# A new order in the projections of a gated mix of two attentions: products, exponentials, splits and copies change places

## The chip, the cores and the metric

The kernel runs on one core of one Trainium2 chip. A core has a matrix engine (TensorE, PE in the profile; its weight loads are PEld), a vector engine (VectorE, DVE), a scalar engine (ScalarE, ACT), a general engine (GpSimd, POOL) and a queue engine that issues transfers (SyncE, SP). Each engine works through its own instructions in order and waits where an operand or a buffer is not ready. The metric is the time of one execution in device microseconds, the median of the runs of a kernel.

## The reference

The input is one sequence x of 2048 tokens with 512 features, in float32. Two attentions with 32 heads of 16 features are computed of it and mixed by a gate.

```python
x = A_x
g = _sigmoid((x * gate_w).sum(-1, keepdims=True))
a = _A_ref(x, A_wqkv, A_wo)               # softmax over all 2048 keys, then @ wo
b = _B_ref(x, B_wq, B_wk, B_wv, B_wo, B_beta)
return g * a + (1 - g) * b

# _B_ref, four segments of 512 tokens:
for s in range(N):
    logits = jnp.einsum("bhqd,bhkd->bhqk", qs, ks) * scale + mask
    a_dot = softmax(logits) @ vs
    pq = phi(qs)                            # phi(t) = t + 1 where t > 0, else exp(t)
    num = jnp.einsum("bhld,bhde->bhle", pq, M)
    den = jnp.einsum("bhld,bhd->bhl", pq, z)[..., None] + 1e-6
    outs.append(sigmoid(beta) * num / den + (1 - sigmoid(beta)) * a_dot)
    pk = phi(ks)
    M = M + jnp.einsum("bhld,bhle->bhde", pk, vs)
    z = z + jnp.einsum("bhld->bhd", pk)
```

A is a full softmax attention. B has a local softmax within each segment of 512 tokens and a memory M, z, that each segment's queries read and each segment's keys and values then add to. The first segment finds the memory empty.

## The kernel before

**Two stages.** The first stage, the projections, makes q, k and v of both attentions, the memory's products and the gate. It lasts for the first 303 us of the profile. The main stage follows: scores (L1056), maxes of scores (L242, reduced on DVE at L275 and L290), exponentials (ACT, L1079), sums over values (L155), and at the end the output projection. The change lies in the first stage alone.

**Slots.** The first stage is a list of slots. A slot is 12 matmuls of 128x128 by 128x512: four steps of depth 128, each with three products of halves. A float32 operand is split into a high half (a cast on ACT) and a low half (a subtraction on DVE or POOL; `split`, L399 to L403), and of the four products of halves the one of low by low is left out. The function `slot` (L377) issues three matmuls, then whatever functions are posted for place 0, then three more and place 1, and so on to place 3. So the order of the work on every engine is written by hand, as slot and place: `post(slots, place, f)` counts from the present slot, `post_at(n, place, f)` names it. Nothing else orders the work; the engines wait for each other by semaphores, and for a buffer by the tile that it reuses (a tag has so many buffers: q1 and q2 three, ph four, full and am two, mn, ex and dn one).

**A's keys and values.** Each pair of chunks of 512 tokens goes through Strassen and Winograd's seven products p1 to p7 (the table `ORDER`, L453; `v_pair` and `k_pair`). S1 to S4 are sums of blocks of x (`s_sum`, L594), T1 to T4 sums of blocks of weights (`t_sum`, L605), and each is split in two halves. In the first `v_pair` the eight tiles of A's queries fill slots 4 to 11, between p2 and the third product. Then come `k_pair` at slot 22 and 29 and two more pieces of `v_pair` to slot 49. With S0 = 50 begin 32 slots of B's q and k tiles, four of q and four of k for each of the four segments.

**A q or k tile** (`qk_tile`, L411). After its slot, ACT copies the bank to the tile full (L426), casts q1 out of it (L427), and POOL makes mn = min(full, 0) (L431); at the next place DVE makes the low half q2 (L434) and, where phi is wanted, ACT makes ex = exp(mn) (L438); one slot on DVE makes ph = max(full, 0) + ex (L443).

**The memory.** `mem_k` transposes a tile of phi(k) (L841, copied by ACT at L843), `mem_k2` multiplies it with v (L855), `mem_k3` adds to the running memory on DVE (L862 to L866). `mem_q` multiplies phi(q) with the memory into four banks, num (L814), and one, den (L818). ACT copies the num banks to tiles (L824) and SP stores them to numd (L825). These tiles take the tags full and am in turn, so they share full's two buffers with the q and k tiles.

**Maxes.** `some_max` does a set of four maxes of the main stage early: four matmuls (L242) into the banks sm, and four reductions on DVE (L275); 96 maxes, 24 sets, are done so. num uses the banks of the same tag sm.

**Gate.** `load_gate` brings four tiles of x's rows, `gate_logit` (L777) sums them on DVE, and `gates` (L899 to L906) transposes the logits, takes the sigmoid and stores them to gd.

**Rows of ones.** Each of the ten tiles of keys gets two small transfers of ones (L765), issued by POOL's queue.

Of the kernel before, what the change touches and what calls it, by code (L numbers as in the profile page):

```python
# [22 lines left out]
CH = 512  # L23
# [24 lines left out]
def gated_mix(ctx, tc, x, xT, wqkv, a_wo, b_wq, b_wk, b_wv, b_wo, beta, gate_w, out):  # L48
# [284 lines left out]
    with ExitStack() as p0:  # L333
# [78 lines left out]
        def qk_tile(w, xc, o, dst, then=None, side="B", bank=None, low=V):  # L412
# [20 lines left out]
            def e1():  # L433
                low.tensor_sub(q2, full, q1.bitcast(F32))  # L434
                store(1, q2)
                if then:
                    ph["ex"] = wk1.tile([128, CH], F32, tag="ex", name="ex")
                    nc.scalar.activation(ph["ex"], ph["mn"], AF.Exp)  # L438
# [7 lines left out]
            post(0, 1, e1)  # L446
            post(1, 1, e2)
# [5 lines left out]
        ORDER = (("p1", "11", "11"), ("p2", "12", "21"), ("p6", "S2", "T2"), ("p7", "S3", "T3"), ("p5", "S1", "T1"),  # L453
# [60 lines left out]
        def v_pair(xo, cs, bs, fill=None, tags=("full", "full", "am", "am")):  # L514
# [42 lines left out]
            for p, x, w in ORDER:  # L557
                x, w = xo[x], vops[w]
                if fill and p == "p6":
                    fill()  # L560
                prods = []
                for b, xb, yb in zip(bs, xbanks, ybanks):
                    if p == "p1":
                        X[b] = xb()
                    elif p in ("p2", "p7"):
                        Y[b] = yb()
                first = p in ("p1", "p2", "p7")
                outer = fill and p in ("p1", "p2")
                order = [(b, k, a, c) for k in range(2) for a, c in ((0, 0), (0, 1), (1, 0)) for b in bs] if outer else \
                    [(b, k, a, c) for b in bs for k in range(2) for a, c in PARTS]  # L570
                left = {b: 6 for b in bs}
                for i in range(0, len(order), 12):
                    part = order[i:i + 12]
                    prods = []
                    for m, (b, k, a, c) in enumerate(part):
                        ps = X[b] if p in ("p1", "p6", "p5", "p3") else Y[b]
                        left[b] -= 1
                        prods.append((ps, x[a][k][:, b * 128:(b + 1) * 128], w[c][k], first and left[b] == 5, left[b] == 0))
                        if left[b] == 0:
                            post(0, m // 3, lambda p=p, b=b: done(p, b))  # L580
                    slot(prods, not first)
# [57 lines left out]
        for n, place, f in ((6, 3, lambda: t_sum("T1", *vb, V)), (7, 0, lambda: t_sum("T3", *vb, P)),  # L639
                            (7, 1, lambda: s_sum("S1", x0, x1, V)), (7, 2, lambda: t_sum("T2", *vb, V)),  # L640
                            (7, 3, lambda: s_sum("S3", x0, x1, P)), (8, 2, lambda: s_sum("S2", x0, x1, V)),
                            (9, 0, lambda: t_sum("T4", *vb, P)), (9, 1, lambda: op_split(vops["T2"], vr[1][2:4], P)),
                            (9, 2, lambda: op_split(xo0["S2"], x0, V)), (10, 0, lambda: s_sum("S4", x0, x1, V)),
                            (10, 1, lambda: op_split(xo0["S3"], x1, V)), (10, 3, lambda: op_split(vops["T3"], vr[1], P)),
                            (11, 1, lambda: op_split(xo0["S1"], x1[2:4], V)), (11, 3, lambda: op_split(xo0["S4"], x0[2:4], V)),
                            (12, 2, lambda: late_op("T1", 2, vr[0][0:2])), (13, 2, lambda: late_op("T4", 3, vr[0][2:4]))):
            post_at(n, place, f)
# [14 lines left out]
        post_at(14, 1, load_k_raw)  # L662
# [41 lines left out]
        for n, place, f in ((18, 3, a22), (19, 2, lambda: s_sum("S1", x2raw, x3raw, V)),  # L704
                            (19, 3, lambda: s_sum("S3", x2raw, x3raw, P)),
                            (24, 2, lambda: plain("11", 7, x2raw[0:2])), (25, 0, lambda: s_sum("S2", x2raw, x3raw, V)),
                            (25, 2, lambda: plain("12", 9, x2raw[2:4])), (26, 0, lambda: s_sum("S4", x2raw, x3raw, V)),
# [32 lines left out]
        staged(xchunk(1), xcs, 1, at_u(8), (6, 10), (47, 0), [(53 + k, 0) for k in range(KT)], P)  # L740
        staged(xchunk(2), xcs, 2, at_u(2), (3, 4), (S0 + 4, 0), [(S0 + 9 + k, 0) for k in range(KT)], P)
        staged(xchunk(3), xcs, 3, at_u(8), (7, 10), (S0 + 10, 0), [(S0 + 17 + k, 0) for k in range(KT)], P)
# [37 lines left out]
        def load_gate(c):  # L780
            t = unit4((3, 7, 2, 2)[c], F32)
# [27 lines left out]
        def mem_q(c):  # L809
# [11 lines left out]

            def keep(i):
                am = wk.tile([128, CH], F32, tag=("full", "am")[i % 2], name="am", bufs=2)
                nc.scalar.copy(am, banks[i])  # L824
                nc.sync.dma_start(numd[c][i], am)  # L825
# [55 lines left out]
        for n in range(36, S0):  # L881
# [3 lines left out]
            elif n > 37:  # L885
                post_at(n, 3, some_max)
# [4 lines left out]
        for n in range(32):  # L891
            if n in (14, 22, 30):
                post_at(S0 + n, 3, lambda c=n // 8: mem_q(c))
            elif n % 2 == 0:
                post_at(S0 + n, 3, some_max)

        def gates():
            gps = me_ps.tile([128, CH], F32, tag="me", name="gps")
            nc.tensor.transpose(gps[:16, :128], glog, identf)  # L899
            gt = wk1.tile([128, 4, 128], F32, tag="ex", name="gt")  # L900
# [437 lines left out]
    n = 0  # L1338
# [81 lines left out]
```

## Time and profile before

| what | value |
|---|---|
| runs | 1770.07, 1770.28, 1775.54 us; median 1770.28 us |
| the profiled execution's own time | 1768.32 us |
| its span, first to last instruction | 1766.5 us |
| mean granted clock of TensorE | 0.995 |
| busy share of the span | PE 98%, PEld 50%, DVE 91%, ACT 82%, POOL 44% |
| first stage, 0 to 303.1 us: busy | PE 277.01, DVE 205.88, ACT 159.17, POOL 143.61 us |
| 400 to 800 us: busy | PE 400.00, DVE 399.78, ACT 356.85, POOL 177.83 us |

The shares over the span are nearly all main stage, in which PE and DVE are busy without a gap. The first stage is read by itself, from the busy times of stretches, from the waits of each engine within it, and from PE's timeline, in which a number in brackets is the idle time ahead of an instruction and the engine and line that ended it. The chain that ended last has 92% of the span in PE.

### The profile page before, as it was taken

What the parts mean: (1) busy time and instruction counts of PE and PEld (TensorE: products, weight loads), DVE (VectorE), ACT (ScalarE), POOL (GpSimd) and SP (SyncE); (2) the same over time, 40 slices, a digit from 0 to 9 for tenths busy, and PEclk for the clock granted to TensorE, in tenths of its full rate; (3) what the DMA queues carried; (4) which work ended last, traced back from release to release, by engine and by line L of the source; (5) the groups of instructions that cost most, each with busy time, mean ns of one, the idle gap of its engine ahead of it and who ended that gap; (6) DMA issues with size and microseconds to landing.
All of it is one profiled execution on the core that took longest, in us unless ns stands there. A gap on an engine that the chain in (4) does not pass through costs nothing.

```text
span 1766.5 us, 41587 instructions
## 1 busy us (share of the span) xinstructions
PE 1735.9 (98%) x15157; PEld 880.9 (50%) x15157; DVE 1599.9 (91%) x3321; ACT 1445.3 (82%) x2779; POOL 770.4 (44%) x1014
## 2 busy tenths in 40 slices
PE   8999988999999999999999999999999999999999
PEld 7876655544444444444444444444444444444444
DVE  7658765999999999999999999999999999999931
ACT  6553546888888888888888888889889888888884
POOL 3533663415162527453445344353434353535343
PEclk9999999999999999999999999999999999999999
DMA  6568876444363436544444444444544444544551
GB/s 234 178 231 222 286 236 206 129 108 137 113 169 107 132 120 183 147 139 137 132 138 127 147 129 147 129 137 115 151 119 146 129 136 124 148 125 142 140 166 62
DMA packets 168507, 264.97 MB, mean 150 GB/s; under 512 B 39496, under 2 KB 80488, under 8 KB 168304
## 3 DMA queue, kind: packets, MB, share of 16 engines
q1 hardware_dynamic: 166720, 260.91, 49.4%
q8 instruction: 121, 1.98, 0.5%
q0 software_dynamic: 1440, 1.14, 0.3%
q14 instruction: 82, 0.67, 0.1%
q10 hardware_dynamic: 144, 0.26, 0.1%
HBM read 177.74 MB, written 83.25 MB: 148 GB/s over the span
## 4 chain that ended last, share of the span: by engine, by line
PE 92%; POOL 2%; ACT 2%; issue 1%; DVE 1%; DMA 1%; SPq 0%; ACTq 0%; POOLq 0%; DVEq 0%
PE ops L155 40%; PE st L1056 27%; PE sm L242 14%; PE pr L385 6%; PE pair L385 2%; PE sm L155 2%; POOL mn L431 1%; DMA numd<-am 1%; POOL u L403 0%; PE mt_ps L232 0%; ACT u L402 0%; PE sm L1056 0%; ACT full L426 0%; PE idle L346 0%; ACT pt L843 0%
## 5 line engine op out<-in xcount | busy, mean ns | idle before, releaser
L1079 ACT ACTIVATE p<-st 128x512 f32<-128x512 f32 x2261 | 1190.9, 601 | 146.9 <-PE sm L242 91.1
L275 DVE TENSOR_REDUCE pm<-sm 128x1 f32<-128x512 f32 x2048 | 1276.9, 684 | 12.1 <-PE sm L242 11.5
L242 PE MATMUL sm<-kA,qA 48*128 48x512 f32 x2048 | 661.4, 424 | 2.3 <-DMA kA<-kdA 2.3
L1056 PE MATMUL st<-qA,kA 50*128 50x512 f32 x2014 | 657.5, 432 | 3.2 <-ACT full L426 3.2
L155 PE MATMUL ops<-p,vA 128*17 128x256 f32 (+3 forms) x6360 | 552.9, 445 | 0.0
L1056 PEld LDWEIGHTS st<-qA,kA 50*128 50x128 f32 x2014 | 327.4, 185 | 426.9 <-ACT p L1079 382.3
L242 PEld LDWEIGHTS sm<-kA,qA 48*128 48x128 f32 x2048 | 338.0, 185 | 12.9 <-issue 2.8
L1180 POOL TENSOR_TENSOR rcp<-rec,minus 128x32 f32<-128x32 f32 x43 | 234.8, 5461 | 78.8 <-DMA rec<-dend 73.1
L290 DVE CUSTOM_DVE_ANT_0 rest<-sm,mask 128x128 f32<-128x128 f32 (+3 forms) x512 | 246.9, 482 | 0.4 <-PE sm L242 0.4
L155 PEld LDWEIGHTS ops<-p,vA 128*17 128x17 f32 x6360 | 129.3, 96 | 214.9 <-issue 183.9
L1060 POOL TENSOR_SCALAR_AFFINE_SELECT p<-p 128x512 f32<-128x512 f32 x128 | 79.4, 636 | 269.4 <-ACT p L1079 264.9
L242 PE MATMUL sm<-kB,qB 48*128 48x128 f32 (+3 forms) x512 | 166.5, 385 | 0.0
L385 PE MATMUL pr<-u,u 128*128 128x512 f32 x392 | 103.4, 403 | 12.7 <-ACT full L426 12.6
L1056 PE MATMUL st<-qB,kB 50*128 50x512 f32 (+1 forms) x495 | 105.4, 329 | 0.3 <-ACT mt L235 0.3
L1056 PEld LDWEIGHTS st<-qB,kB 50*128 50x128 f32 x495 | 68.6, 186 | 62.2 <-ACT p L1079 50.4
L385 PEld LDWEIGHTS pr<-u,u 128*128 128x128 f32 x392 | 72.9, 191 | 33.2 <-ACT full L426 15.2
L155 PE MATMUL ops<-p,vB 128*17 128x128 f32 (+3 forms) x1504 | 88.3, 350 | 0.2 <-ACT part L1270 0.2
L214 POOL TENSOR_TENSOR dm<-pm 128x32 f32<-128x32 f32 x32 | 7.6, 239 | 172.1 <-DVE pm L275 172.1
L242 PEld LDWEIGHTS sm<-kB,qB 48*128 48x128 f32 x512 | 80.2, 185 | 0.0
L434 DVE TENSOR_TENSOR q<-full,q 128x512 fp32r<-128x512 f32 x40 | 32.2, 805 | 33.9 <-ACT q L427 30.7
L223 POOL CAST ms<-pm 128x16 fp32r<-128x16 f32 x32 | 6.3, 196 | 126.7 <-DVE pm L290 126.6
L431 POOL TENSOR_SCALAR mn<-full 128x512 f32<-128x512 f32 x24 | 40.2, 1674 | 38.1 <-ACT full L426 37.8
(230 smaller groups left out, 1496.1 us busy)
## 6 DMA issues: line engine op xcount, KB each, us to landing
kA<-kdA SPq DMA_DIRECT2D x256, 128.0 KB
vA<-vdA SPq DMA_DIRECT2D x31, 544.0 KB
kA<-kdA SPq DMA_DIRECT2D x256, 64.0 KB
qB<-qdB SPq DMA_DIRECT2D x192, 64.0 KB
kB<-kdB SPq DMA_DIRECT2D x192, 64.0 KB
kdA<-q SPq DMA_DIRECT2D x32, 256.0 KB
qA<-qdA SPq DMA_DIRECT2D x64, 128.0 KB
qdB<-q SPq DMA_DIRECT2D x32, 256.0 KB
```

The lines of the kernel that those rows point to most:

```text
L155: behind[0] = nc.tensor.matmul(*args, **kw)
L214: nc.gpsimd.tensor_sub(dm, pm[:, :, :, 2:4], pm[:, :, :, 0:2])
L242: nc.tensor.matmul(ps[:, n0:n0 + n], rows(qt[u][:, :, s * 128:(s + 1) * 128], h, 48), rows(k[:, :, k0:k0 + n], h, 48), start=True, stop=True)
L275: nc.vector.tensor_reduce(pm[:, h, s, kc:kc + 1], ps, axis=AX.X, op=ALU.max, negate=True)
L290: nc.vector.tensor_tensor_reduce(out=tri["rest"][:, 0:w], in0=ps[:, n0:n0 + w], in1=tri["mask"][:, CH - w:], scale=-1.0, scalar=3.0e38, op ...
L385: nc.tensor.matmul(ps, l, r, start=start, stop=stop, skip_group_check=chained)
L431: nc.gpsimd.tensor_scalar_min(ph["mn"], full, 0.0)
L434: low.tensor_sub(q2, full, q1.bitcast(F32))
L1056: nc.tensor.matmul(ps[:, n0:n0 + CH - q0], rows(k[:, :, b * 128:(b + 1) * 128], h, 50), rows(q[:, :, q0:], h, 50), start=True, stop=True)
L1060: nc.gpsimd.affine_select(out=x, in_=x, pattern=[[0, 4], [1, 128]], base=0, channel_multiplier=-1, compare_op=ALU.is_ge, fill=0.0)
L1079: nc.scalar.activation(p[:, h], ps, AF.Exp, scale=SCALE)
L1180: eng.tensor_tensor(r, rec, minus, op=ALU.pow)
```

## The change

Nothing that is computed changes, and no product is added or left out. What changes is the place of the work, and at four points its engine, its tile or its bank:

- The third of the seven products is p7 (S3 by T3), then p6 (S2 by T2). S and T sums and their splits get new slots and places to match, and S3's sum goes from POOL to DVE.
- In the first `v_pair`, p1 and p2 no longer end all four banks in the last four matmuls: the first half of the depth is done for all banks, then the second half bank by bank. The queries take their banks in the other order.
- The load of raw k, one plain split and one sum move by a slot or a place; the sets of maxes begin at slot 39, not 38, and the 13 sets within the last 32 slots stand at every even slot from 0 to 24.
- phi's exponential moves from place 1 to place 3, behind the next tile's copy and cast.
- The low halves of x's chunks 1, 2 and 3 move from POOL to DVE and from place 0 to place 2; chunk 3 is loaded four slots later, into other tiles.
- The twenty transfers of ones go to SP's queue.
- Two of the loads of gate rows come later and into other tiles; the gates are made at slot 26 of the 32, not 30, and in the tag gw, not ex.
- The memory's products leave by four tiles of their own, not by full and am, and `mem_q` stands one slot earlier, at 13, 21 and 29.

```diff
             def e1():
                 low.tensor_sub(q2, full, q1.bitcast(F32))
                 store(1, q2)
+
+            def e1x():
                 if then:
                     ph["ex"] = wk1.tile([128, CH], F32, tag="ex", name="ex")
                     nc.scalar.activation(ph["ex"], ph["mn"], AF.Exp)
...
             post(0, 1, e1)
+            post(0, 3, e1x)
             post(1, 1, e2)
...
-        ORDER = (("p1", "11", "11"), ("p2", "12", "21"), ("p6", "S2", "T2"), ("p7", "S3", "T3"), ("p5", "S1", "T1"),
+        ORDER = (("p1", "11", "11"), ("p2", "12", "21"), ("p7", "S3", "T3"), ("p6", "S2", "T2"), ("p5", "S1", "T1"),
                  ("p3", "S4", "22"), ("p4", "22", "T4"))
...
-                if fill and p == "p6":
+                if fill and p == "p7":
                     fill()
...
-                order = [(b, k, a, c) for k in range(2) for a, c in ((0, 0), (0, 1), (1, 0)) for b in bs] if outer else \
+                order = [(b, 0, a, c) for a, c in ((0, 0), (0, 1), (1, 0)) for b in bs] + \
+                    [(b, 1, a, c) for b in bs for a, c in PARTS] if outer else \
                     [(b, k, a, c) for b in bs for k in range(2) for a, c in PARTS]
...
-                            (7, 3, lambda: s_sum("S3", x0, x1, P)), (8, 2, lambda: s_sum("S2", x0, x1, V)),
...
+                            (7, 0, lambda: t_sum("T3", *vb, P)), (7, 1, lambda: s_sum("S3", x0, x1, V)),
+                            (7, 3, lambda: op_split(xo0["S3"], x1, V)), (8, 0, lambda: op_split(vops["T3"], vr[1], P)),
...
-        post_at(14, 1, load_k_raw)
+        post_at(15, 0, load_k_raw)
...
-        staged(xchunk(2), xcs, 2, at_u(2), (3, 4), (S0 + 4, 0), [(S0 + 9 + k, 0) for k in range(KT)], P)
-        staged(xchunk(3), xcs, 3, at_u(8), (7, 10), (S0 + 10, 0), [(S0 + 17 + k, 0) for k in range(KT)], P)
+        staged(xchunk(2), xcs, 2, at_u(2), (3, 4), (S0 + 4, 0), [(S0 + 9 + k, 2) for k in range(KT)], V)
+        staged(xchunk(3), xcs, 3, at_u(2), (10, 8), (S0 + 14, 0), [(S0 + 18 + k, 2) for k in range(KT)], V)
...
-                post_at((S0 - 10 if i < 4 else S0 + 10) + i, 1 + 2 * r, lambda t=t, r=r: nc.gpsimd.dma_start(
+                post_at((S0 - 10 if i < 4 else S0 + 10) + i, 1 + 2 * r, lambda t=t, r=r: nc.sync.dma_start(
...
-                    qk_tile(wq8, xq, o, qd["A", o, c], side="A", bank=(me_bank, pr_bank)[o // 2])
+                    qk_tile(wq8, xq, o, qd["A", o, c], side="A", bank=(pr_bank, me_bank)[o // 2])
...
+            ams = unit4(7, F32)
+
             def keep(i):
-                am = wk.tile([128, CH], F32, tag=("full", "am")[i % 2], name="am", bufs=2)
-                nc.scalar.copy(am, banks[i])
-                nc.sync.dma_start(numd[c][i], am)
+                nc.scalar.copy(ams[i], banks[i])
+                nc.sync.dma_start(numd[c][i], ams[i])
...
-            elif n > 37:
+            elif n > 38:
                 post_at(n, 3, some_max)
...
-            if n in (14, 22, 30):
+            if n in (13, 21, 29):
                 post_at(S0 + n, 3, lambda c=n // 8: mem_q(c))
-            elif n % 2 == 0:
+            elif n % 2 == 0 and n < 26:
                 post_at(S0 + n, 3, some_max)
...
-            post_at(S0 + (2, 8, 14, 20)[c], 2, lambda c=c: load_gate(c))
-        post_at(S0 + 30, 1, gates)
+            post_at(S0 + (2, 8, 16, 21)[c], 2, lambda c=c: load_gate(c))
+        post_at(S0 + 26, 2, gates)
```

Three places show how the instructions move. First POOL, from its first sum to its last low half of the T blocks, in the first `v_pair`. In the rows L605 (now L609) is a sum of T blocks, L594 one of S blocks, L403 a pair of low halves; u_255 and u_256 are the low halves' tiles of T2 and T3. Before:

```order
L605 TENSOR_TENSOR u_245<-u_245 128x512 x2
L594 TENSOR_TENSOR u_247<-u_246,u_247 128x512 x2
L756 DMA gh<-beta 16x4x1 x8
L605 TENSOR_TENSOR u_244<-u_244,u_245 128x512 x2
L403 TENSOR_TENSOR u_255<-u_245,u_255 128x512 x2
L403 TENSOR_TENSOR u_256<-u_245,u_256 128x512 x2
L403 TENSOR_TENSOR u_626<-u_244,u_626 128x512 x2
L403 TENSOR_TENSOR u_647<-u_244,u_647 128x512 x2
```

With the change:

```order
L609 TENSOR_TENSOR u_245<-u_245 128x512 x2
L403 TENSOR_TENSOR u_256<-u_245,u_256 128x512 x2
L760 DMA gh<-beta 16x4x1 x8
L609 TENSOR_TENSOR u_244<-u_244,u_245 128x512 x2
L403 TENSOR_TENSOR u_255<-u_245,u_255 128x512 x2
L403 TENSOR_TENSOR u_640<-u_244,u_640 128x512 x2
L403 TENSOR_TENSOR u_659<-u_244,u_659 128x512 x2
```

T3's low halves stand right behind T3's sum, ahead of the transfers of gh; T2's keep their place behind T4's sum, and S3's sum is gone from this queue.

Second ACT, at the memory's first products, slots 63 to 66. L426 is a copy out of a bank, L427 the cast to q1, L438 (now L440) phi's exponential, L824 (now L829) the copies of num. Before:

```order
L426 COPY full<-pr 128x512
L427 CAST q_2302<-full 128x512
L438 ACTIVATE ex<-mn 128x512
L824 COPY am<-num 128x512 x4
L426 COPY full<-pr 128x512
L427 CAST q_2373<-full 128x512
L438 ACTIVATE ex<-mn 128x512
L829 ACTIVATE dn<-den,eps 128x512
L843 COPY pt<-tps 128x512
```

With the change:

```order
L426 COPY full<-pr 128x512
L427 CAST q_2252<-full 128x512
L829 COPY u_2301<-num 128x512 x4
L440 ACTIVATE ex<-mn 128x512
L426 COPY full<-pr 128x512
L427 CAST q_2313<-full 128x512
L834 ACTIVATE dn<-den,eps 128x512
L235 CAST mt<-mt_ps 32x128
L440 ACTIVATE ex<-mn 128x512
```

The exponential of a tile has moved behind whatever else stands between its cast and the next tile's copy, here the copies of num, which now go to tiles of the kind u and no longer to am and full.

Third DVE, at the same place, from a set of maxes on. L275 are the four reductions of a set, L777 (now L781) a gate logit, L443 (now L445) phi's last step, L434 a tile's low half. Before:

```order
L275 TENSOR_REDUCE pm<-sm 128x1 x4
L777 SCALAR_TENSOR_TENSOR jk,glog<-u_1984,gw 128x512
L443 SCALAR_TENSOR_TENSOR ph<-full,ex 128x512
L434 TENSOR_TENSOR q_2276<-full,q_2275 128x512
L443 SCALAR_TENSOR_TENSOR ph<-full,ex 128x512
L434 TENSOR_TENSOR q_2303<-full,q_2302 128x512
L443 SCALAR_TENSOR_TENSOR ph<-full,ex 128x512
L434 TENSOR_TENSOR q_2374<-full,q_2373 128x512
```

With the change:

```order
L403 TENSOR_TENSOR u_2022<-u_1801,u_2021 128x512
L275 TENSOR_REDUCE pm<-sm 128x1 x4
L781 SCALAR_TENSOR_TENSOR jk,glog<-u_1966,gw 128x512
L445 SCALAR_TENSOR_TENSOR ph<-full,ex 128x512
L434 TENSOR_TENSOR q_2253<-full,q_2252 128x512
L445 SCALAR_TENSOR_TENSOR ph<-full,ex 128x512
L434 TENSOR_TENSOR q_2314<-full,q_2313 128x512
L275 TENSOR_REDUCE pm<-sm 128x1 x4
```

A low half of x's third chunk (u_2022, L403) stands in DVE's queue just ahead of the reductions, and the next set's reductions follow after two tiles, where before they follow after four; the memory's first products lie in between.

More of the change, by code (lines that the diff above doesn't have):

```diff
@@ L638, in late_op @@
             op_split(vops[name], src, P)
-        for n, place, f in ((6, 3, lambda: t_sum("T1", *vb, V)), (7, 0, lambda: t_sum("T3", *vb, P)),
-                            (7, 1, lambda: s_sum("S1", x0, x1, V)), (7, 2, lambda: t_sum("T2", *vb, V)),
-                            (7, 3, lambda: s_sum("S3", x0, x1, P)), (8, 2, lambda: s_sum("S2", x0, x1, V)),
[L642 to L646, printed above, removed]
+        for n, place, f in ((6, 1, lambda: s_sum("S1", x0, x1, V)), (6, 3, lambda: t_sum("T1", *vb, V)),
+                            (7, 0, lambda: t_sum("T3", *vb, P)), (7, 1, lambda: s_sum("S3", x0, x1, V)),
+                            (7, 3, lambda: op_split(xo0["S3"], x1, V)), (8, 0, lambda: op_split(vops["T3"], vr[1], P)),
+                            (8, 1, lambda: t_sum("T2", *vb, V)), (8, 3, lambda: s_sum("S2", x0, x1, V)),
+                            (10, 0, lambda: t_sum("T4", *vb, P)), (9, 3, lambda: s_sum("S4", x0, x1, V)),
+                            (10, 1, lambda: op_split(vops["T2"], vr[1][2:4], P)), (10, 2, lambda: op_split(xo0["S2"], x0, V)),
+                            (12, 1, lambda: op_split(xo0["S1"], x1[2:4], V)), (13, 1, lambda: op_split(xo0["S4"], x0[2:4], V)),
+                            (13, 2, lambda: late_op("T1", 2, vr[0][0:2])), (14, 2, lambda: late_op("T4", 3, vr[0][2:4]))):
             post_at(n, place, f)
@@ L706, in gated_mix @@
                             (24, 2, lambda: plain("11", 7, x2raw[0:2])), (25, 0, lambda: s_sum("S2", x2raw, x3raw, V)),
-                            (25, 2, lambda: plain("12", 9, x2raw[2:4])), (26, 0, lambda: s_sum("S4", x2raw, x3raw, V)),
+                            (26, 0, lambda: plain("12", 9, x2raw[2:4])), (26, 1, lambda: s_sum("S4", x2raw, x3raw, V)),
                             (26, 2, lambda: op_split(xo1["S2"], x2raw, V)), (27, 2, lambda: op_split(xo1["S3"], x3raw, V)),
@@ L739, in gated_mix @@
         staged(b_wk, wB, "k", at_u(4), (9, 5), (45, 0), [(48 + k, 3) for k in range(KT)], P)
-        staged(xchunk(1), xcs, 1, at_u(8), (6, 10), (47, 0), [(53 + k, 0) for k in range(KT)], P)
-        staged(xchunk(2), xcs, 2, at_u(2), (3, 4), (S0 + 4, 0), [(S0 + 9 + k, 0) for k in range(KT)], P)
-        staged(xchunk(3), xcs, 3, at_u(8), (7, 10), (S0 + 10, 0), [(S0 + 17 + k, 0) for k in range(KT)], P)
+        staged(xchunk(1), xcs, 1, at_u(8), (6, 10), (47, 0), [(53 + k, 2) for k in range(KT)], V)
+        staged(xchunk(2), xcs, 2, at_u(2), (3, 4), (S0 + 4, 0), [(S0 + 9 + k, 2) for k in range(KT)], V)
+        staged(xchunk(3), xcs, 3, at_u(2), (10, 8), (S0 + 14, 0), [(S0 + 18 + k, 2) for k in range(KT)], V)
         vB = {}
@@ L780, in load_gate @@
         def load_gate(c):
-            t = unit4((3, 7, 2, 2)[c], F32)
+            t = unit4((3, 7, 6, 6)[c], F32)
             for b in range(4):
@@ L899, in gates @@
             nc.tensor.transpose(gps[:16, :128], glog, identf)
-            gt = wk1.tile([128, 4, 128], F32, tag="ex", name="gt")
+            gt = wk1.tile([128, 4, 128], F32, tag="gw", name="gt")
             nc.scalar.activation(gt[:16, 0], gps[:16, :128], AF.Sigmoid)
```

## The prediction

> **What bounds the kernel now.** I read the busy times of stretches first, because they show where the matrix engine is short of work. In each row stand the stretch in microseconds, its length, the busy time (and instructions) of PE, PEld, DVE, ACT and POOL, the granted clock, the share of the DMA engines and GB/s.
>
> ```profile
> 0.00:303.10 303.10, 277.01 (x1661) 207.70 (x1661) 205.88 (x330) 159.17 (x287) 143.61 (x159) 0.98 0.71 226
> ...
> 41.10:53.10 12.00, 8.92 (x24) 6.61 (x25) 12.00 (x13) 5.54 (x10) 7.86 (x5) 0.72 0.26 97
> 121.70:125.00 3.30, 0.99 (x5) 0.48 (x4) 0.34 (x1) 1.10 (x2) 3.21 (x4) 1.00 0.91 247
> 164.80:303.10 138.30, 120.58 (x995) 85.63 (x993) 88.80 (x159) 75.29 (x134) 74.28 (x72) 0.98 0.74 241
> ...
> 202.90:220.80 17.90, 13.71 (x118) 9.84 (x118) 14.07 (x27) 9.82 (x19) 11.48 (x7) 1.00 0.69 218
> 220.80:237.00 16.20, 10.40 (x72) 6.54 (x70) 3.55 (x6) 7.19 (x14) 5.91 (x7) 0.79 0.61 216
> 237.00:260.90 23.90, 22.12 (x224) 16.39 (x224) 21.56 (x37) 12.94 (x24) 19.82 (x18) 1.00 0.79 246
> 260.90:282.00 21.10, 18.35 (x179) 12.30 (x179) 11.06 (x24) 11.74 (x22) 6.15 (x5) 1.00 0.51 188
> 299.10:303.10 4.00, 0.87 (x6) 0.45 (x6) 0.69 (x1) 2.36 (x5) 3.69 (x8) 1.00 0.98 320
> ...
> 400.00:800.00 400.00, 400.00 (x3777) 181.90 (x3775) 399.78 (x849) 356.85 (x692) 177.83 (x250) 1.00 0.49 140
> ```
>
> The main stage (last row) has PE and DVE full; nothing of the change lies there, and the text ahead of it in each queue stays, so it should only begin earlier. The first stage, the projections, lasts 303.1 us with PE busy 277.01: 26.1 us are idle. That is all that a new order can win, with what a lowered clock costs beside it. The second view, PE's waits within 0 to 312 us (total, times, longest), names what ends them:
>
> ```profile
> PE pr L385 <- ACT full L426: 12.6, 8, 5.8
> PE st L1056 <- ACT full L426: 3.2, 2, 2.3
> PE pair L385 <- POOL u L403: 3.0, 2, 2.3
> PE sm L242 <- DMA kA<-kdA: 2.3, 1, 2.3
> ...
> PE pr L385 <- DVE vs L545: 1.3, 1, 1.3
> ```
>
> The first two are banks that ACT has not copied out. The waits of ACT, and of DVE, from 164 to 302 us say why ACT is late:
>
> ```profile
> ACT ex L438 <- POOL mn L431: 28.3, 17, 3.2
> ACT ex L438 <- DVE ph L443: 14.9, 6, 3.1
> ...
> ACT full L426 <- DMA numd<-am: 8.9, 3, 5.1
> ```
> ```profile
> DVE ph L443 <- PE den L818: 7.0, 2, 3.7
> ```
>
> An exponential stands at ACT's head until POOL's minimum is there, with the next copy out of a bank behind it; and three times a copy waits until the memory's products have left their tile. PE's timeline gives prices (start, duration, count, idle ahead and its releaser):
>
> ```profile
> 43.96 0.96 PE L385 MATMUL pair<-u,u 128*128 128x512 f32 x3 [2.30 <-POOL u L403]
> 45.65 7.63 PE L385 MATMUL pair<-u,u 128*128 128x512 f32 x20 [0.72 <-POOL u L403]
> 53.12 5.60 PE L385 MATMUL pr<-u,kA 128*128 128x512 f32 x24
> 58.56 11.04 PE L385 MATMUL pair<-u,qtmp 128*128 128x512 f32 x48
> ...
> 127.95 0.73 PE L242 MATMUL sm<-kA,qA 48*128 48x512 f32 x4
> 128.62 3.02 PE L385 MATMUL pr<-u,qtmp 128*128 128x512 f32 x12
> 131.56 0.73 PE L242 MATMUL sm<-kA,qA 48*128 48x512 f32 x4
> ...
> 232.33 4.70 PE L385 MATMUL pr<-u,u 128*128 128x512 f32 x12 [5.80 <-ACT full L426]
> ```
>
> Two slots take 58.56 − 53.12 = 5.44 us, so a slot is 2.72; with a set of maxes it is 131.56 − 127.95 = 3.61, so a set costs 0.89.
>
> **The change part by part.** *Banks freed one by one.* The fourth row of causes, 1.3 us at p1 and p2, goes: each bank now ends three matmuls (0.68 us) after the one before, and its copy follows it. Term −1.3; no gain at worst, no more than 1.3 at best.
>
> *Third product.* The stretch 41.10 to 53.10 is p6: 24 matmuls in 12.00 us instead of 5.44, so 6.56 are lost, 3.0 idle and the rest to a clock of 0.72. p7 now stands there. These are the rows of POOL, and of DVE, from which its operands are timed:
>
> ```profile
> 34.69 4.33 POOL L756 DMA_DIRECT2D gh<-beta  x8
> 39.03 3.21 POOL L605 TENSOR_TENSOR u<-u,u 128x512 f32<-128x512 f32 x2
> 42.20 6.76 POOL L403 TENSOR_TENSOR u<-u,u 128x512 fp32r<-128x512 f32 x4
> ...
> 240.81 1.92 POOL L431 TENSOR_SCALAR mn<-full 128x512 f32<-128x512 f32 x1
> ```
> ```profile
> 31.82 1.77 DVE L434 TENSOR_TENSOR q<-full,q 128x512 fp32r<-128x512 f32 x1
> ...
> 35.82 0.68 DVE L434 TENSOR_TENSOR q<-full,q 128x512 fp32r<-128x512 f32 x1
> ...
> 237.50 2.49 DVE L275 TENSOR_REDUCE pm<-sm 128x1 f32<-128x512 f32 x4
> ...
> 241.31 1.08 DVE L443 SCALAR_TENSOR_TENSOR ph<-full,ex 128x512 f32<-128x512 f32 x1
> ```
>
> T3's sum is POOL's first in both orders and its low halves now follow at once, two of 6.76 / 4 = 1.69 us; DVE makes S3 and its split: all is there near 36 us, before PE reaches the place (41.1 less 1.3). The DMAs of gh (4.33), T4's sum (3.21) and T2's two low halves (3.4) then end near 46, while p6, two slots later, starts near 45: about 0.4 us of waiting is left. Smaller waits appear behind it, since POOL's pairs of splits are still one chain and ACT casts ahead of its copies:
>
> ```profile
> 53.16 1.14 ACT L402 CAST u<-u 128x512 fp32r<-128x512 f32 x2 [1.23 <-DVE qtmp L403]
> ```
>
> I take 1.0 for p5 (the casts of late T1, 1.14 a pair, now stand ahead of copies out of p6's banks), 1.5 for p3 (its banks' copies stand behind the casts of raw k, whose load waits until POOL has made T4's low halves, two of 1.69 us, out of the same tiles) and 0.7 for T3's operands of k; behind each wait stands only the next product, on PE. Bounds 0 and 6.6, the whole stall merely moved. Term −6.6 + 3.6 = −3.0.
>
> *A set of maxes one slot later, raw k one slot later.* The 2.3 us at 121.7 end with a load of kA. The set moved behind it takes its 0.89 in a later slot, so nothing is won or lost by that. Term −2.3 (bounds 0 and −2.3).
>
> *The exponential behind the copy; low halves from POOL to DVE; the products in their own tiles.* These act together on the 32 slots from 164.8. Idle there is 4.19 + 5.80 + 1.78 + 2.75 + 3.13 = 17.65 us by the rows of stretches, and the 12 matmuls at 232.33 took 4.70 where 3.02 is usual: 1.7 more. In all 19.3. The biggest piece is seen in three rows of SP's queue and ACT:
>
> ```profile
> 226.87 2.66 SPq L825 DMA_DIRECT2D numd<-am  x4
> ```
> ```profile
> 224.54 2.02 ACT L824 COPY am<-num 128x512 f32<-128x512 f32 x4
> 231.69 0.58 ACT L426 COPY full<-pr 128x512 f32<-128x512 f32 x1 [5.13 <-DMA numd<-am]
> 232.31 0.62 ACT L427 CAST q<-full 128x512 fp32r<-128x512 f32 x1
> ```
>
> ACT had copied the four products by 226.6 and needed the tile back: 5.13 us until their DMA had landed. With tiles of their own the copies out of banks wait for none of it. The exponential at place 3 is issued behind the next copy and cast (0.58 and 0.62); it is itself later by half a slot, and ph with it, which only the memory's products read, a slot or more on. Its minimum also loses the low halves that stood ahead of it on POOL.
>
> What is new: 12 low halves on DVE, at 0.68 each alone and 1.77 beside a POOL sum of two inputs. Beside the minimum (POOL's 240.81, DVE's 241.31) DVE took 1.08 and POOL 1.92. I take 1.0 each, 12 us, on a DVE that was busy for 88.80 of 138.30 us and now gets about 124: room on average, not everywhere. The memory products now stand one slot behind a set of maxes, not two: their banks wait for four reduces (2.49) and DVE's phi behind these. PE reaches them 0.67 + 2.95 us after the set begins; reduces end about 3.0 after it, then logits and phi for 0.68 each or more: 1 to 2.5 us late, twice, 4.0 in all, with the next slot's matmuls standing behind the first of them on PE. The gates at slot 26 are transposed behind their logits, and their activations stand ahead of a copy on ACT: 1.0. The loads of gate rows and of x's last chunk go to other tiles with as many issues on SP; their readers are DVE's logits and ACT's casts, slots later: nothing, and 1.0 if DVE's logits run late, which the DVE rival holds. Against 19.3 stand 5.0: term −14.3 (bounds −19.3 and −3).
>
> *Twenty small DMAs from POOL to SP.* POOL is spared their issue; SP's own issue is 2.66 / 4 = 0.67 us where it waits and less elsewhere, one or two a slot of 2.72 to 3.61, beside two stores. It fits; cost nothing, and SP's backlog is a rival below.
>
> Sum: −1.3 − 3.0 − 2.3 − 14.3 = −20.9, say **−21**. The profiled execution took 1768.32 us with a span of 1766.5, so a span of about 1745.5 and 1747.3 us as its time; the median of the runs shown is 1770.28, 2.0 above, so **1749 us**.
>
> **The rivals.** *DVE becomes the bound where x is split and maxes run.* For: in 202.90 to 220.80 it is busy 14.07 us already, PE 13.71; four low halves more are 2.7 at 0.68 and 7.1 at 1.77. Against: part of the 14.07 is the stretching by POOL's low halves that leave. Two such places: between 1 and 14 us; with 7, 1756. The Trainium skill, SBUF — State Buffer, § Who interferes with whom, says that a DVE instruction with two SBUF inputs and a GpSimd instruction reading SBUF exclude each other, the second standing until the first has ended: it speaks against this move, since by it a low half could stand for a whole minimum. The trace does not bear out the full block: 1.08 beside 1.92, where a wait for the rest of the minimum would have ended later.
>
> *The early gain is given back.* p5, p3 and k's products wait for POOL and raw k as long as p6 did, 6.6 instead of 3.6 us, and one such gap lowers the clock again as at 45.65: +4 to +5, so 1753. For: POOL's chain is as long as before. Against: three products stand between, 16 us of cover.
>
> *The main stage does not begin earlier.* Its first keys, gates and values come by DMA, and from 299.10 the DMA engines are at 0.98. If they hold it, the last 14.3 are lost: 1764. Against: 0.74 of 138.30 us is 102 us of transfers, which fit into 124.
>
> *Slower: SP's queue.* Each of ten tiles of keys gets two of the small DMAs on SP; if such a DMA must wait until the tile's maxes have been read, the stores of q and k behind it wait, then the buffers of q1 (three, so two slots, 7.2 us of cover), the cast and the bank. A hold of three slots, 10.8 us, leaves 3.6 us exposed, ten times: +36, so 1785. It decides from a hold of about 9.8 us, where 10 × 2.6 eats the 21 and a little more. For: the trace has DVE and ACT waiting for stores at times. Against: none of PE's waits above comes from POOL's issues of these DMAs.
>
> **How the numbers follow.** Forecast 0.55 (own range 1743 to 1755), DVE 0.17, early gain given back 0.13, main stage held 0.09, slower 0.06. All costs of new waits at nothing give −29.5: 1740.8, so the low end is 1740; the high end, 1762, takes in both middle rivals with the clock's 3 us, and nearly the held stage. Under 0.3% (5.3 us) this measurement can't tell from none: 1765 to 1775.6. Faster: the first three and a third of the fourth, 0.88; the rest of the fourth 0.06; slower 0.06.
>
> **What would show it.** The stretch near 40 us has PE full at clock 1.00; no wait of PE names numd or 5.8 us; ACT's exponential waits less than half of 28.3 + 14.9; the first st starts near 281. Wrong: PE waits of over 2 us for DVE near slots 59 to 72, DVE over 0.95 busy there, q1 waiting for stores, or a first st that starts early and then waits for loads.

## The result and the profile after

The changed kernel takes 1757.53 us (median of four runs, 1757.03 to 1758.45); the kernel before, on the same chip, 1770.17 us. The ratio is 0.9923 with a 95% interval of 0.9903 to 0.9943: faster, by 12.6 us where 21 were forecast. That is inside the stated range of 1740 to 1762 us, and above the forecast's own 1743 to 1755. The profiled execution has a span of 1755.3 us, 11.2 less than before.

The busy times of stretches, columns as before: the first stage, the stretch of p7 to p3, the 32 slots of B, and one stretch of these.

```profile
0.00:292.50 292.50, 279.25 (x1661) 205.00 (x1661) 207.07 (x344) 159.52 (x287) 110.16 (x125) 0.99 0.74 234
39.40:66.20 26.80, 23.71 (x98) 17.54 (x97) 15.12 (x19) 13.16 (x27) 16.00 (x16) 1.00 0.52 168
...
161.26:292.50 131.24, 125.38 (x999) 85.81 (x997) 92.87 (x175) 75.51 (x134) 48.54 (x48) 0.97 0.79 253
...
241.00:257.00 16.00, 12.73 (x70) 5.75 (x68) 8.02 (x14) 7.54 (x14) 2.78 (x3) 0.79 0.84 272
```

The main stage is what it was (1462.8 us of the span lie behind the first stage, 1463.4 before); 10.6 of the 11.2 us are a first stage of 292.5 instead of 303.1 us. PE's waits in it (total, times, longest) are others than before:

```profile
PE num L818 <- DVE pm L275: 3.3, 1, 3.3
PE pair L385 <- ACT vt L528: 2.2, 3, 1.3
PE gps L904 <- DVE spare L869: 1.8, 1, 1.8
PE pair L385 <- ACT full L482: 1.4, 1, 1.4
PE pr L385 <- DVE vs L548: 1.4, 1, 1.4
...
PE pr L385 <- ACT full L426: 1.0, 3, 0.5
```

The waits for copies out of banks have fallen from 12.6 and 3.2 us to 1.0, and none is for the products' transfers. In their place stand the memory's products waiting for DVE (num, at the second of three), and four smaller ones. PE's timeline gives the places (17.61 is the first query, 46.59 lies in p6, 66.19 is the end of p3):

```profile
17.61 0.39 PE L385 MATMUL pr<-kA,qtmp 128*128 128x512 f32 x1
...
46.59 5.07 PE L385 MATMUL pair<-u,u 128*128 128x512 f32 x21 [0.37 <-DVE u L403]
...
64.68 1.67 PE L385 MATMUL pair<-u,qtmp 128*128 128x512 f32 x6 [1.30 <-ACT vt L528]
66.19 5.60 PE L385 MATMUL pr<-u,kB 128*128 128x512 f32 x24
...
144.59 1.62 PE L385 MATMUL pr<-u,qtmp 128*128 128x512 f32 x6 [1.44 <-DVE vs L548]
...
210.31 3.60 PE L818 MATMUL num<-ph,mbd 32*32 32x512 f32 x32
...
247.58 4.93 PE L818 MATMUL num<-ph,mbd 32*32 32x512 f32 x32 [3.27 <-DVE pm L275]
252.44 1.43 PE L822 MATMUL den<-ph,zbd 128*32 128x512 f32 x8
...
292.55 1.16 PE L1367 MATMUL ops<-identf 128*128 128x128 f32 x8
```

The 0.37 us ahead of p6 end with S2's low halves on DVE, at 43.07 + 3.46 = 46.53. T2's on POOL were ready before, at 45.98; side by side the four took some 1.7 us each, where a low half alone takes DVE 0.68:

```profile
42.56 3.42 POOL L403 TENSOR_TENSOR u<-u,u 128x512 fp32r<-128x512 f32 x2
```
```profile
43.07 3.46 DVE L403 TENSOR_TENSOR u<-u,u 128x512 fp32r<-128x512 f32 x2
```

The 32 products of num took 1.14 us before. Now the first set takes 3.60, the second has 3.27 us of idle ahead of it and takes 4.93, with a granted clock of 0.50 from 247.6 to 252.4: 2.5 and some 7 us lost. The first set waits in its midst, for the banks that the four reductions read and then for phi, which stands behind them on DVE:

```profile
209.11 2.47 DVE L275 TENSOR_REDUCE pm<-sm 128x1 f32<-128x512 f32 x4
...
212.11 0.68 DVE L445 SCALAR_TENSOR_TENSOR ph<-full,ex 128x512 f32<-128x512 f32 x1
```

What was late at the second is seen on three engines. First SP, whose rows from 232 to 244 us follow each other without a pause (start, time of the issues, count):

```profile
232.12 0.65 SPq L769 DMA_DIRECT2D kA<-qtmp  x1
232.81 1.80 SPq L177 DMA_DIRECT2D kA<-kdA  x4
234.66 4.79 SPq L174 DMA_DIRECT2D qB<-qdB  x6
239.49 2.75 SPq L174 DMA_DIRECT2D kB<-kdB  x6
242.35 0.36 SPq L423 DMA_DIRECT2D qdB<-q  x1
242.75 0.65 SPq L769 DMA_DIRECT2D kA<-qtmp  x1
243.51 0.34 SPq L423 DMA_DIRECT2D qdB<-q  x1
```

Then ACT, and then DVE:

```profile
238.51 0.57 ACT L426 COPY full<-pr 128x512 f32<-128x512 f32 x1
244.61 0.62 ACT L427 CAST q<-full 128x512 fp32r<-128x512 f32 x1 [5.54 <-DMA qdB<-q]
```
```profile
245.63 0.69 DVE L434 TENSOR_TENSOR q<-full,q 128x512 fp32r<-128x512 f32 x1 [4.10 <-DMA qdB<-q]
246.24 0.69 DVE L403 TENSOR_TENSOR u<-u,u 128x512 fp32r<-128x512 f32 x1
246.84 2.48 DVE L275 TENSOR_REDUCE pm<-sm 128x1 f32<-128x512 f32 x4
```

A store of q (L423) is issued at 242.35, behind a row of loads and a transfer of ones. The cast and the low half, which need the stored tile back, wait 5.54 and 4.10 us, the four reductions stand behind the low half on DVE, and the products need the banks that these reductions read. From 219 to 250 us SP's rows are never half a microsecond apart (waits of its own, 4.6 us in all, are inside them), and twelve of its instructions are the transfers of ones.

### The profile page after: what moved, and what is told of

The parts are those of the page before. It is cut to its first block, busy times and chain, and to the rows that moved or that the text cites. A ratio compares the mean times of both kernels' runs of the same rounds, so it can differ in the third digit from the quotient of the medians.

```text
span 1755.3 us, 41552 instructions
## 1 busy us (share of the span) xinstructions
PE 1737.1 (99%) x15157; PEld 877.7 (50%) x15157; DVE 1600.7 (91%) x3335; ACT 1445.4 (82%) x2779; POOL 737.1 (42%) x980
## 4 chain that ended last, share of the span: by engine, by line
PE 92%; DVE 3%; DMA 1%; ACT 1%; issue 1%; SPq 0%; POOL 0%; DVEq 0%; ACTq 0%; POOLq 0%
PE ops L155 40%; PE st L1061 28%; PE sm L242 14%; PE pr L385 6%; PE sm L155 2%; PE pair L385 1%; DVE pm L275 1%; DVE q L434 1%; DVE u L403 1%; PE num L818 0%; PE mt_ps L232 0%; DMA u<-wqkv 0%; DVE u L598 0%; PE sm L1061 0%; SPq L174 0%
## 5 line engine op out<-in xcount | busy, mean ns | idle before, releaser
L275 DVE TENSOR_REDUCE pm<-sm 128x1 f32<-128x512 f32 x2048 | 1276.4, 683 | 13.4 <-PE sm L242 12.7
L155 PEld LDWEIGHTS ops<-p,vA 128*17 128x17 f32 x6360 | 129.1, 96 | 214.8 <-issue 183.7
L1201 POOL TENSOR_TENSOR v<-v,inv 128x512 f32<-128x512 f32 x31 | 39.9, 1286 | 28.2 <-DMA inv<-rdA 21.9
```

The costliest lines, as they stand in the source:

```text
L155: behind[0] = nc.tensor.matmul(*args, **kw)
L275: nc.vector.tensor_reduce(pm[:, h, s, kc:kc + 1], ps, axis=AX.X, op=ALU.max, negate=True)
L1201: eng.tensor_mul(k["v"], k["v"], k["inv"])
```

## The experiments

The theory to be tested was S: SP's queue, given ten pairs of small transfers, holds the stores of q and k, and so the buffers of the halves, ACT and DVE. Its rivals were D (the products stand one slot behind a set of maxes and wait for its reductions whatever SP does) and L (the low halves overload DVE). Differences between kernels below are those of medians against the changed kernel's 1757.53 us, unless the kernel before is named. The kernels ran beside several sets of runs of the kernel before, whose medians were 1769.15 to 1770.46 us, so about 1 us of a difference can come from that.

**Ones back on POOL.**

```diff
-    lambda t=t, r=r: nc.sync.dma_start(raw(t)[64 * r + 48:64 * r + 50], ...)
+    lambda t=t, r=r: nc.gpsimd.dma_start(raw(t)[64 * r + 48:64 * r + 50], ...)
```

> The changed kernel with one part undone: the twenty small transfers of ones are issued by POOL again. Theory S (SP's queue): the second memory products came 7 us late because SP, which issues without a pause from 219 to 250 us, held the stores of q behind ten of these transfers at about 0.65 us each and a row of loads; with them on POOL the cast to q1 no longer waits 5.5 us, the products come 1 to 2 us late, and the kernel gets 4 to 6 us faster than the changed kernel's 1757.5, about 1752.5. Theory D (DVE's reductions of the set ahead of the products are what is late): nothing moves by more than 1 us, or it gets slower by a little since POOL's minimum waits for the issues.

Measured: 1753.24 us (1752.08 to 1754.24), 4.3 less; 0.9907 of the kernel before (0.9891 to 0.9924, which overlaps the changed kernel's interval). All its runs lie below all runs of the changed kernel. Each taken against its own runs of the kernel before, 3.4 us lie between them. PE's timeline, and ACT's at the cast that waited 5.54 us:

```profile
210.47 3.62 PE L818 MATMUL num<-ph,mbd 32*32 32x512 f32 x32
...
245.27 4.07 PE L818 MATMUL num<-ph,mbd 32*32 32x512 f32 x32 [0.79 <-DVE pm L275]
```
```profile
242.62 0.62 ACT L427 CAST q<-full 128x512 fp32r<-128x512 f32 x1 [3.33 <-DMA qdB<-q]
```

S holds, for a part: the cast's wait falls to 3.33 us, with the twelve loads of B's queries and keys still ahead of the store, and the second products lose 3.7 us instead of 7.1. In the profiled executions the main stage's first copy comes at 289.22 instead of 292.55, 3.3 us sooner, which is just what the second products gained. The first products' 2.5 us are untouched, so D has its share too.

**Low halves back on POOL.**

```diff
-[(53 + k, 2) for k in range(KT)], V)      # chunk 1; chunks 2 and 3 alike
+[(53 + k, 0) for k in range(KT)], P)
```

> The changed kernel with one part undone: the low halves of x's chunks 1 to 3 on POOL at place 0, as before. Theory L (12 low halves overload DVE): DVE is relieved by 8 us around the memory products and the kernel gets 3 to 6 us faster, about 1753. Theory S (SP's queue) and the prediction: POOL's minimum comes 1.3 to 1.7 us later in 8 slots, phi's exponential waits again and holds the next tile's work on ACT, though behind its copy; 0 to 4 us slower, about 1759.

Measured: 1762.58 us (1762.07 to 1763.30), 5.0 slower. L falls, by more than the other side had expected. Engine and place go back together here, so their shares are not told apart. ACT's waits from 156 to 295 us and PE's timeline show the exponential's old cause again:

```profile
ACT ex L440 <- POOL mn L431: 14.5, 9, 5.0
```
```profile
211.75 4.53 PE L385 MATMUL pr<-u,u 128*128 128x512 f32 x12 [3.56 <-ACT full L426]
...
252.19 4.94 PE L818 MATMUL num<-ph,mbd 32*32 32x512 f32 x32 [3.21 <-DVE pm L275]
```

In the changed kernel the exponential's wait is 3.0 us in all. The second products wait as long for DVE's reductions as they do with the low halves on DVE (3.21 us here, 3.27 in the changed kernel). The low halves ahead of POOL's minimum hold it, the exponential and the next copy, even though one copy now stands ahead of the exponential.

**Old order of products in the two later value pieces.**

```diff
-            for p, x, w in ORDER:
+            for p, x, w in (ORDER if fill else ORDER[:2] + (ORDER[3], ORDER[2]) + ORDER[4:]):
```

> The changed kernel with the old order of products (p6 third, p7 fourth) in the two later value pieces alone; the first piece keeps p7 third. If the wait of 1.4 us for DVE at 144.6 us comes from p7 wanting p2's bank at once, with four reductions ahead of the sum that frees it, that wait goes and the kernel gets 1.4 us faster, about 1756. If it comes from something else on DVE, no change.

Measured: 1758.48 us (1757.18 to 1759.30), no difference. The wait of 1.44 us at 144.6 is gone, so its cause was p7, which begins a bank of its own right behind p2, while p6 adds to the bank of p1. The time did not follow. PE's timeline, the row of the first wait after it and the two sets of products:

```profile
187.26 3.06 PE L385 MATMUL pr<-u,u 128*128 128x512 f32 x12 [0.38 <-ACT full L426]
...
210.32 3.61 PE L818 MATMUL num<-ph,mbd 32*32 32x512 f32 x32
...
248.10 4.93 PE L818 MATMUL num<-ph,mbd 32*32 32x512 f32 x32 [3.77 <-DVE pm L275]
```

The first products come at 210.32, as in the changed kernel (210.31). Whatever PE gained had been lost by then.

**Memory products one slot later**, at 14, 22, 30, with the sets of maxes on the even slots that are left.

```diff
-            if n in (13, 21, 29):
+            if n in (14, 22, 30):
...
-            elif n % 2 == 0 and n < 26:
+            elif n % 2 == 0 and n < 29:
```

> The changed kernel with the memory products at slots 14, 22 and 30 again, and the sets of maxes where they were before, so that two slots lie between a set and the products. Theory D (the products wait for the four reductions of the set one slot ahead): their waits, 2.4 and 7 us, fall to under 1 us each and the kernel gets 5 to 8 us faster, about 1751. Theory S (SP's queue holds q's stores, and so DVE): the first products' 2.4 us go, the second still waits for most of its 7 us; 2 to 3 us faster, about 1755.

Measured: 1758.98 us (1757.45 to 1760.07), no gain. All three sets of products run in 1.14 us without a wait, so D was right on what they wait for; but a new wait eats it. DVE's timeline and PE's:

```profile
264.88 0.69 DVE L781 SCALAR_TENSOR_TENSOR jk<-u,gw 128x512 f32<-128x512 f32 x1 [9.46 <-DMA kdB<-q]
```
```profile
266.33 1.09 PE L846 MATMUL tps<-identf,ph 128*128 128x128 f32 x4 [5.80 <-DVE ph L445]
```

A gate logit writes its product, which nobody reads, to the tile in which the denominators leave (the tag dn); with the products later, DVE comes to this logit at 255.4 us instead of 261.0, while SP sends the denominators when it did (260.16 us, 260.40 in the changed kernel). So DVE stands for 9.46 us instead of 4.18. The trace names the last transfer of SP's queue that it saw, a store of k; that it is the tile of the denominators is shown by two kernels below, with and without the logit's edit, which differ in that tile alone.

**Single parts on the kernel before.** First the products' own tiles (with the third chunk and the gate rows moved to free them):

```diff
+            ams = unit4(7, F32)
             def keep(i):
-                am = wk.tile([128, CH], F32, tag=("full", "am")[i % 2], name="am", bufs=2)
-                nc.scalar.copy(am, banks[i])
-                nc.sync.dma_start(numd[c][i], am)
+                nc.scalar.copy(ams[i], banks[i])
+                nc.sync.dma_start(numd[c][i], ams[i])
```

> The kernel before with one part of the change alone: the memory's products leave by four tiles of their own (and, to free these tiles, the third chunk of x and two loads of gate rows go where and when the change puts them, the low halves staying on POOL). If the three waits for the products' transfers (5.80, 1.46 and 2.27 with 0.92 us on PE, and 1.7 of lowered clock) were time of their own, they all go: 10 to 12 us faster, about 1759. If the exponential that waits for POOL's minimum would have held ACT there anyway, half of it: about 1764.

Measured: 1760.67 us, 0.9943 of the kernel before (0.9922 to 0.9965): some 10 us faster, near the larger of the two gains expected. The slot that had waited 5.80 us now waits 0.57 (PE's timeline):

```profile
227.35 3.02 PE L385 MATMUL pr<-u,u 128*128 128x512 f32 x12 [0.57 <-ACT full L426]
```

Second the exponential behind the copy:

```diff
+            def e1x():
                 if then:
                     ph["ex"] = ...
...
+            post(0, 3, e1x)
```

> The kernel before with one part alone: phi's exponential behind the next tile's copy and cast. The prediction's reasoning: PE's waits for copies that stood behind an exponential, 1.35, 0.54, 0.81, 1.01, 0.74 and 0.90 us, go and the three waits for the products' transfers stay: 4 to 5 us faster, about 1765. If the exponential's own lateness (and phi's) is felt by the memory products: no change, about 1769.

Measured: 1774.87 us (ten runs), 1.0020 of the kernel before (1.0008 to 1.0032): slower, which neither expectation held. ACT's timeline, then DVE's and PE's:

```profile
222.59 1.07 ACT L827 COPY am<-num 128x512 f32<-128x512 f32 x2 [1.96 <-DVE ph L445]
229.95 1.07 ACT L827 COPY am<-num 128x512 f32<-128x512 f32 x2 [6.29 <-DMA numd<-am]
```
```profile
231.58 0.69 DVE L445 SCALAR_TENSOR_TENSOR ph<-full,ex 128x512 f32<-128x512 f32 x1 [8.42 <-ACT ex L440]
```
```profile
232.94 5.10 PE L385 MATMUL pr<-u,u 128*128 128x512 f32 x12 [7.76 <-ACT full L426]
```

The last reader of full is phi on DVE. With the exponential later, the products' copies find full taken; two of the four go out, the other two wait until the first two have landed, and the exponential stands behind them. The wait of 5.80 us has become 7.76.

Third the early part, the first product order with all its new places:

```diff
-        ORDER = ((...p2...), ("p6", "S2", "T2"), ("p7", "S3", "T3"), ...
+        ORDER = ((...p2...), ("p7", "S3", "T3"), ("p6", "S2", "T2"), ...
+        # with the new places of sums and splits, the banks and the load of raw k
```

> The kernel before with the early part alone: third product, banks of the first two products and of the queries, the new places of sums and splits, raw k one slot later. By the trace of the changed kernel the first set of maxes comes 1.9 us earlier; the wait of 2.3 us for its keys stays where it was unless the load is early enough, and the new 1.4 us wait in the last value piece comes on top: 0 to 2 us faster, about 1768.5. The prediction had 4.3 us here: about 1765.

Measured: 1771.15 us (ten runs), 1.0002 of the kernel before (0.9992 to 1.0012): nothing. PE's timeline names what took the gain in one execution, the slowest of the ten (1774.34 us):

```profile
88.26 1.65 PE L385 MATMUL pair<-qtmp,kA 128*128 128x512 f32 x6 [1.44 <-ACT full L479]
...
122.33 1.44 PE L242 MATMUL sm<-kA,qA 48*128 48x512 f32 x4 [2.40 <-DMA kA<-kdA]
123.70 5.42 PE L385 MATMUL pr<-u,kA 128*128 128x512 f32 x12
...
150.88 1.60 PE L385 MATMUL pr<-u,qtmp 128*128 128x512 f32 x6 [1.44 <-DVE vs L545]
```

PE reaches the first set of maxes at 119.93 (122.33 less 2.40), 1.9 us sooner than before, and 1.44 of that goes to p2's bank. In this execution the clock takes more: behind the wait of 2.40 us it is 0.50 to 0.52 until 129.1, and the slot takes 5.42 us. In the profile before, the same slot behind a wait of 2.31 us took 3.01, at a clock of 1.00; in the profiles of the two kernels above it took 4.61 us behind 2.03 and 2.21. How many of the other executions lose this is not shown. The changed kernel has no wait there, and its four runs lie within 1.4 us, where those of the kernel before spread over 8; that the one comes of the other is argued, not shown.

**Both causes together**, ones on POOL and the products one slot later, with the logit's product written over its own input:

```diff
-            jk = wk1.tile([128, D], F32, tag="dn", name="jk")
-            nc.vector.scalar_tensor_tensor(jk, xg, 1.0, gw[0], ...
+            nc.vector.scalar_tensor_tensor(xg, xg, 1.0, gw[0], ...
```

> The changed kernel with three things: ones on POOL's queue again, memory products at slots 14, 22, 30 with the sets where they were before, and the gate logits' unused product written over its own input, so that it waits for no transfer of the denominators. If SP's queue is the root and the set one slot ahead of the products the second cause, the products wait for nothing and the memory part loses 2 to 3 us in all: 8 to 10 us faster than the changed kernel, about 1748.5. If something further holds the q stores (the loads of 12 pieces of B's queries and keys on SP), 4 us faster only, about 1753, as with the ones alone.

Measured: 1747.26 us (1746.99 to 1747.84), 10.3 less than the changed kernel and 0.9865 of the kernel before (0.9847 to 0.9883). Two kernels leave out one of the three edits each:

> The changed kernel with ones on POOL's queue and the memory products at slots 14, 22 and 30, the gate logits' unused product in its old tile, which the denominators' transfer must leave first. If SP's queue was what made the logit wait 9.5 us with the products moved alone, that wait shrinks to some 4 us and half or more of it is covered: 6 to 8 us faster than the changed kernel, about 1750. If the tile is a cause of its own, it stays: about 1753, and the whole rest of the gain of the kernel with all three came from the logits.

> The changed kernel with ones on POOL's queue and the logits' product over its own input, the memory products one slot behind a set of maxes as the change has them. The logit's wait of 4.4 us for the denominators goes; if it is what delays the gates' transpose (1.9 us on PE), that goes: 1 to 2 us faster than with the ones alone, about 1751.5. The products' waits of 2.4 and 3.4 us stay if the place behind the set is their cause; they are what separates this from the kernel with all three (1747.3): 4 to 5 us.

Measured: 1755.07 us without the logit's edit, 1751.51 with the products one slot early. So next to the other two the logit's tile is worth 7.8 us, and the place of the products 4.3, as far as single medians tell. In the first of them the logit still waits 9.38 us (DVE's timeline), although SP is rid of the ones:

```profile
262.05 0.69 DVE L781 SCALAR_TENSOR_TENSOR jk<-u,gw 128x512 f32<-128x512 f32 x1 [9.38 <-DMA kdB<-q]
```

The tile is a cause of its own, then. Theory S had expected for that kernel a wait of some 4 us and a gain of 6 to 8; the wait stayed, and 2.5 us were gained, less than with the ones alone. The other kernel came out as expected (1751.5): its second products still wait 1.70 us for DVE's reductions.

**The order of the later value pieces once more**, on the kernel with the three edits (the diff is the one above).

> The kernel with all three, and p6 third in the two later value pieces. Alone on the changed kernel this took away PE's 1.4 us wait at 144.6 us and the time did not move. If the gain was lost there because SP's queue and not PE set when the second products came, it arrives here, where that backlog is gone: 1.4 us faster, about 1745.9. If another wait takes it anyway (stores, buffers of q1): no change, 1747.3.

Measured: 1746.37 us (1745.94 to 1746.48), 0.9859 of the kernel before (0.9844 to 0.9875), the fastest kernel of all. It is 0.9 below the kernel with three edits, whose interval against the kernel before overlaps; its runs all lie below the other's, but the two were not run side by side. That most of the 1.4 us arrives once the later waits are gone fits this; it isn't settled.

**The exponential back at place 1**, on the kernel with the three edits.

```diff
-            post(0, 3, e1x)      # and the exponential issued in e1 again
```

> The kernel with all three (ones on POOL, products one slot later, logits in place), and phi's exponential back at place 1, ahead of the next tile's copy. Alone on the kernel before, the exponential behind the copy made it 2 to 4 us slower, because phi, and with it the release of the tile full, came later while full was also held by the products' transfers. If that was the reason, it is a gain where the products have tiles of their own: without it this kernel is 3 to 6 us slower than 1747.3, about 1751.5. If the exponential's place costs in itself, this kernel is faster, about 1744.

Measured: 1755.92 us (1755.30 to 1758.29), 8.7 slower than with it at place 3. PE's and ACT's waits from 156 to 300 us:

```profile
PE pr L385 <- ACT full L426: 6.1, 7, 1.4
```
```profile
ACT ex L438 <- DVE ph L443: 25.1, 10, 3.3
ACT ex L438 <- POOL mn L431: 14.2, 13, 1.5
```

With the exponential at place 3 these three are 1.9, 16.3 and 3.3 us. The same move costs 0.2% in the kernel before, where the products share full, and gains 8.7 us here, where they have tiles of their own. So of the two kernels tried it pays only in this one, while the tiles pay alone, some 10 us. The two kernels differ in more than the tiles; that the sharing turns the sign is read from the trace of the kernel above with the exponential alone, and no edit isolates it.

## Why the prediction was right in part

The direction, the place and the mechanism of the main gain were right; the sum was 1.7 times too large. That the time is inside the range is owed to the rivals, by which its high end was set. Up to the main stage's first copy the sum is 10 us off, 4.0 ahead of slot 50 and 6.0 in the 32 slots. Of the signs named, ACT's exponential waits fell to 11.3 + 3.0 us and no wait names numd; but the first st starts at 291.38, not near 281, and two of the signs of being wrong came: PE waits 3.27 us for DVE behind slot 71, and q1 waits for stores.

- *Banks freed one by one*, −1.3: right. The queries, which need the banks, begin at 17.61 instead of 18.95.
- *Third product*, −3.0: p7 found its operands. p6 waits 0.37, and that 0.4 were foretold is luck: they were foretold of T2, and it waits for S2's low halves, which the prediction did not time. The eight slots from p7 to p3 take 26.80 us instead of 8 × 2.72 = 21.76: 5.0 are lost where I took 2.9, most of it in p5 and p3, and k's pair loses 1.44 instead of 0.7. By the early part alone, PE is 1.9 us ahead at the first set of maxes, not 4.3, so this term was −0.6. With k's pair 6.5 us are lost where the sum had 3.6 and the rival "the early gain is given back" 6.6: in size it is the rival that happened. The means had been named in the sum, ACT's copies behind casts that wait for raw k (1.76 us for its load, ahead of the copy that PE awaits at 64.68), and priced too low. The new 1.4 us at p2's bank, for p7 begins a bank where p6 added to one, was missed altogether: the prediction followed the new order through the first value piece and not through the two later ones.
- *The set of maxes one slot later*, −2.3: right, the wait is gone. What the clock loses behind it in some executions was in no term.
- *The 32 slots*, −14.3 (−13.4 with the set moved into them): from slot 50 to the main stage's first copy (L1362, now L1367) it was 303.46 − 164.8 before and is 292.55 − 161.3 now, 7.4 less. The removed 19.3 did go. What failed is the size of what is new, 5.0: the products lost 2.5 and 7.1 where 4.0 in all were taken, and the gates 1.75 instead of 1.0. The reductions were to end 3.0 us after their set begins; at the first products they end 4.9 us after it (211.58 less 206.70), for DVE had a logit, phi and two low halves ahead of them. At the second, the stores are added.
- *Twenty small DMAs*, nothing: this is the step that was wrong. They cost 3.3 us by the profiles and 4.3 by the medians, and these lie within the 7.1 of the second products. The prediction counted the ones and two stores a slot, which fit on average; it left out the loads, which come in rows, sixteen of them ahead of the store at 242.35, and with twelve of the ones in the same stretch there was no room to catch up. The slower rival had the way from stores to buffers of q1 and the cast, and put its price at waits for key tiles that never came: the twelve issues took 0.63 to 0.72 us each. The Trainium skill, DMA: Bandwidth & Descriptors, § Issuing engines are not separate DMA queues, says that spreading transfers over engines saves just the sequencer's time to issue them, usually small next to the transfer. The trace agrees that an issue takes its queue's time, 0.65 us on SP and 0.59 on POOL with the ones back there; no run times such a transfer to its landing. Small as one issue is, the row of them was not.
- *Low halves on DVE*: the rival that DVE becomes the bound fell. Taking them back costs 5.0 us; POOL's minimum then waits, and the exponential with it.
- *The exponential*: right in this kernel and in its mechanism, but under a condition that the prediction had not seen: the products must not share full. Alone on the kernel before, the move made it slower.

## What to carry to other kernels

A full queue is judged in its densest stretch, not on its average: ask what stands in one row ahead of the store that frees a buffer. A buffer shared by two uses makes their delays add up, and an unused output in a shared tile is a wait like any other; give such outputs a place that nobody else needs before moving instructions. Two edits that rest on the same buffer can't be priced one by one: one of them was worth +0.2% alone and −8.7 us in a kernel that has the other.

## What the runs showed of the hardware

Behind the wait of 3.27 us at the memory's products the granted clock was 0.50 for 4.8 us, 0.79 over 241 to 257, and products of 1.14 us took 4.93 with their own waits in it. Waits of nearly one length did not act alike: behind 2.40 us at the first set of maxes the clock fell to 0.50, behind 2.31 us, in another kernel's execution, it stayed at 1.00. On SP the issues that did not wait differ by form: 0.33 to 0.36 us for a store of 128x512, 0.42 for a load of a piece of B's keys (0.46 from one to the next) and 0.65 for a pair of rows of ones.
